# Edges of a GraphSAGE layer sorted into buckets in three parts of 32, 20 and 16 buckets a row instead of two of 41 and 27, with the sort in four portions and two parts merged under the sums

## The chip, the cores and the metric

The kernel runs on one core of a Trainium2 chip. The metric is the device time of one execution in microseconds (us); lower is better. The core's engines are called here as the profile calls them: PE (matmuls; PEld is its weight load), DVE (the vector engine), ACT (the scalar engine), POOL (GpSimd, which here issues the gathers) and SP (which issues most plain DMAs).

## The reference

```python
N, deg, D = 12500, 64, 64;  E = N * deg            # 800,000 edges
nsum = segment_sum(x[src], dst, N)                 # rows of x, added up by destination
return x @ w_self + (nsum * deg_inv[:, None]) @ w_neigh
```

`src` and `dst` are random and unordered, so the kernel has to bring the edges into an order in which TensorE can add them.

## The kernel before, in words

**Keys and sort.** Each edge becomes one 32-bit key (`make_keys`), made so that keys in order stand by bucket: a bucket is one block of 144 destinations (two halves of 72) and one of 98 blocks of 128 sources. There are 87 x 98 = 8526 buckets. The edges lie as 128 rows of 6250 keys, one row per lane. `sort_runs` sorts each row with a list of compare steps (`GAPS`): a minimum and a maximum on DVE per step (L223, L227; several instructions where the shape is ragged), and an ACT copy of the keys that have no partner (L229). The last 30 steps (`APART`) are cut into portions by position: keys below `SPLIT` first, then those below `CUT1`, then the rest.

**Rows and runs.** The buckets are cut into parts, each of 128 bucket rows: part 0 has 41 buckets a row, part 1 has 27 (`KPRS`). `find_rows` finds where each of a part's 128 bucket rows begins in each sorted row of edges, by one count over a window of keys for each (L454 on ACT with Sign and an accumulator, L456 on DVE, dealt out by `on_act`). The counts are made into offsets (L460, L461), transposed on PE (L463) and written as addresses `ix` (L465). With them `gather_runs` issues 128 indirect DMAs on POOL (L473), each followed by a short memset (`pause`), so that bucket row r lies in lane r as 128 sorted runs of `LENS[part][0]` keys. In part 0 the first `EARLY` = 76 counts stand between the second portion's steps.

**Merging.** `merge_runs` merges the 128 runs in seven rounds; `merge_round` issues its minima and maxima on DVE (L283, then L295 down the distances) with ACT copies of keys without a partner (L279). Part 0 is merged in groups of 32, 32 and 64 runs, the last round (`merge_last`, L312, L327, copies L316) in a lower and an upper piece, so that counting can begin below `LOWER`. Part 1's merge is a generator that the program advances by a number of ns, as an estimate, at a time.

**Buckets.** `find_buckets` and `count_below` find where each bucket begins in its row (part 0 on ACT, L610; part 1 on DVE, L612). `gather_buckets` brings each bucket of part 0 into 178 places `v` by indirect DMA (L633, addresses L644 on DVE); part 1 does the same under the sums (`find_and_gather`, addresses on ACT, L663). `decode_buckets` splits keys into source and destination (DVE, L680 to L685), narrows them to 16 bits (ACT, L690, L694), stores the sources to `sl` and turns the destinations into `dlT` (PE L700, ACT L701). Keys beyond a bucket's 128 places are collected by `leftovers`.

**The sums.** `nodes` runs over 1066 tiles of up to 8 buckets. For each 28 buckets `one_hots` broadcasts `sl` to all lanes (SP, L797, 896 KB) and DVE compares it: `ohs` (sources, L799) and `ohd` (destinations, L802). A tile has 8 matmuls `ct` = rows of x picked by `ohs` (L827), a copy `xg` of them to half precision (L837 on ACT, or L835 on DVE for some tiles from tile `SHARE` = 800), and 16 matmuls that add them by destination into PSUM `acc` (L883). Each 7 blocks of destinations the leftovers come in by one-hots `ohl` (L876) and the sum is copied out (L891, L893) and finished: `po` = sum @ w_neigh (L951), an ACT copy (L952), times the degree and plus the self terms on DVE (L957, L958), stored (L959). Between tiles the program issues the other streams: part 1's merge by 280 ns of estimate a tile, then one of its counts every second tile, then its decoding.

**Order.** `after_sort` and `sums_and_merge` write out this order by hand, and every engine takes its instructions in it. In the sums a DVE instruction thus stands behind all one-hots that the program wrote ahead of it; three `ohs`, five `ohd` and seven `xg` buffers say how far an engine may be ahead.

Of the kernel before, what the change touches and what calls it, by code (L numbers as in the profile page):

```python
# [23 lines left out]
H = 64  # L24
# [7 lines left out]
KPRS = (41, 27)  # L32
ROWS = (128, 128)
BASE = (0, 128 * KPRS[0])
NCOL = 128 * sum(KPRS)
NCNT = [(k + 3) // 4 for k in KPRS]
LENS = ((64, 108, 188, 336, 608, 1144, 2176, 4208),
        (48, 80, 132, 236, 420, 780, 1472, 2824))
# [12 lines left out]
SHARE = 800  # L51
EARLY = 76
SHARED = 0
SPLIT = 2560
# [3 lines left out]
LOWER = 2240  # L58
CLOSE = 32
BEHIND = 6  # L60
NEARLY = 36
LAG = 4
OCT = 7

# [17 lines left out]
class Windows:  # L82


    def __init__(self):
        cum = bid_cum()
        self.w1 = []
        for part in range(2):
# [8 lines left out]
        for part in range(2):  # L97
# [15 lines left out]
CUT1 = max(lo + 2 * n for lo, n in WIN.w1[:128]) + LENS[0][0] + 2  # L113
CUT1 += CUT1 % 2
FROM1 = min(lo for lo, _ in WIN.w1[128:]) - 2
assert max(lo + 2 * n for lo, n in WIN.w1[:EARLY]) <= SPLIT < CUT1 and FROM1 >= 0
# [4 lines left out]
def on_act(c):  # L121

    return c % 13 in (0, 2, 4, 7, 9, 11) or c < EARLY or c >= 128 + SHARED


def on_act2(part):

    return part == 0


def constants():
    thr = bid_base(np.concatenate([BASE[p] + np.arange(ROWS[p]) * KPRS[p] for p in range(2)]))
    act = np.array([on_act(c) for c in range(NC1)])
    t1 = np.where(act, -(thr - 1).view(np.float32), thr.view(np.float32))
    mul = np.where(act, -1.0, 2.0)
    add = np.array([(n if a else 0) + lo - 1 for (lo, n), a in zip(WIN.w1, act)])
    add[128:] -= FROM1
    c1 = np.zeros((128, 3, NC1), np.float32)
    c1[:, 0], c1[:, 1], c1[:, 2] = t1, mul, add
    out = {"c1": c1}  # L140
    for p in range(2):
# [3 lines left out]
        act = np.array([on_act2(p) for k in range(kpr)])  # L145
        first = np.array([lo + (n / 2 + 0.25 if a else 0) for (lo, n), a in zip(WIN.w2[p], act)])
        mid = v | np.uint32(1 << 14)
        c2 = out[f"c2_{p}"] = np.zeros((128, 5, kpr), np.float32)
# [3 lines left out]
        c2[:, 3] = np.where(act, -0.5, 1.0)  # L152
        c2[:, 4] = first + np.arange(128)[:, None] * PITCH2[p]
# [62 lines left out]
def sort_runs(nc, bufs, n):  # L216
# [19 lines left out]
    for last in (SPLIT, CUT1):  # L236
        edge = []
        for (gap, odd) in GAPS[:-APART - 1:-1]:
            last = -(-(last - odd * gap) // (2 * gap)) * 2 * gap + odd * gap
            edge.insert(0, last)  # L240
        edges.append(edge)
    edges = [[0] * APART] + edges + [[n] * APART]
    assert all(x < y for a, b in zip(edges, edges[1:]) for x, y in zip(a, b))
# [95 lines left out]
class Kernel:  # L339
    def __init__(self, tc, ctx, ins, outs):  # L340
# [4 lines left out]
        self.d1 = [self.dram.tile([128, n], F32, name=f"d1_{p}") for p, n in enumerate((CUT1, PITCH1 - FROM1))]  # L345
        self.sl = self.dram.tile([NCOL, 128], BF, name="sl")
        self.xt = self.dram.tile([NB * 128, 128], FH, name="xt")
        self.tops = [self.dram.tile([128, PCS * 9], F32, name=f"tops{p}") for p in range(2)]
        self.lt = [self.dram.tile([CHK, 128], F32, name=f"lt{p}") for p in range(2)]
        self.d2 = [self.dram.tile([128, PITCH2[p]], F32, name=f"d2_{p}") for p in range(2)]  # L350

    def setup(self):
        nc, keep = self.nc, self.keep
        self.c2 = [keep.tile([128, 5, KPRS[p]], F32, name=f"c2_{p}") for p in range(2)]
# [3 lines left out]
        self.cnt = keep.tile([128, sum(NCNT) + 3], F32, name="cnt")  # L358
        nc.gpsimd.memset(self.cnt, 0.0)
        self.deg = keep.tile([FB, 4 * NQ], F32, name="deg")  # L360
# [7 lines left out]
        for p in range(2):  # L368
# [7 lines left out]
        self.wide = keep.tile([128, OCT * HN], FH, name="wide")  # L376
        nc.gpsimd.iota(self.wide, pattern=[[1, OCT * HN]], base=0, channel_multiplier=0,
# [37 lines left out]
    def sort_edges(self, mps):  # L415
# [5 lines left out]
        self.c1 = l1.tile([128, 3, NC1], F32, name="c1")  # L421
        self.prow = [l1.tile([128, 128], F32, name=f"prow{p}") for p in range(2)]
        for p, n in enumerate((CUT1, PITCH1 - FROM1)):
# [6 lines left out]
        with tc.tile_pool(name="raw", bufs=1) as raw:  # L430
            with tc.manual_schedule():
                self.make_keys(raw, a)
                nc.sync.dma_start(self.c1, self.I["c1"])
                for p in range(2):
# [8 lines left out]
    def find_rows(self, part, mps):  # L443
# [3 lines left out]
        junks = [l1.tile([128, 512], BF, name=f"junk{e}") for e in "ad"]  # L447
        c0 = 128 * part
        for c in range(c0, c0 + 128):
# [3 lines left out]
            if on_act(c):  # L453
                nc.scalar.activation(junks[0][:, :n], w, AF.Sign, bias=self.c1[:, 0, c:c + 1], accum_out=a)  # L454
# [13 lines left out]
    def gather_runs(self, part, u):  # L468
# [3 lines left out]
        for p in range(128):  # L472
# [3 lines left out]
            self.pause(1 if part or p >= CLOSE else 2)  # L476

    def merge_runs(self, part, u, pong, sizes):
# [19 lines left out]
        first = 0  # L498
        for n in sizes:
# [5 lines left out]
            first += n  # L505
            while len(done) > 1 and done[-1][0] == done[-2][0]:
# [74 lines left out]
    def self_terms(self, pool, mps):  # L581
# [3 lines left out]
        for b0 in range(0, NB, 8):  # L585
# [8 lines left out]
            for j in range(nb // 2):  # L594
# [3 lines left out]
            nc.sync.dma_start(self.own[b0 * 128:(b0 + nb) * 128].rearrange("(b p) f -> p b f", p=128),  # L598
                              o[:, :nb // 2].rearrange("p a b f -> p (a b) f"))

    def count_below(self, part, k, acc):
# [5 lines left out]
        on = on_act2(part)  # L607
        junk = self.keep.tile([128, max(n for _, n in WIN.w2[0] + WIN.w2[1])], BF, name=f"junk2{part}")
        if on:
            nc.scalar.activation(junk[:, :n], w, AF.Sign, bias=c2[:, 2, k:k + 1], accum_out=acc[:, k:k + 1])  # L610
        else:
            nc.vector.tensor_scalar(junk[:, :n], w, c2[:, 1, k:k + 1], None, op0=OP.is_lt, op1=OP.add,  # L612
                                    accum_out=acc[:, k:k + 1])

    def find_buckets(self, part):
# [12 lines left out]
        nc.vector.tensor_tensor(acc, acc, self.c2[part][:, 3], op=OP.mult)  # L628
        nc.vector.tensor_tensor(acc, acc, self.c2[part][:, 4], op=OP.add)
# [18 lines left out]
    def find_and_gather(self, part, vp):  # L648
# [7 lines left out]
        for k in range(kpr + LAG):  # L656
# [4 lines left out]
            if k >= LAG:  # L661
                g = k - LAG
                nc.scalar.activation(ix[:, g:g + 1], acc[:, g:g + 1], AF.Relu, bias=self.c2[part][:, 4, g:g + 1])  # L663
# [3 lines left out]
    def decode_buckets(self, part, v, vp, mps):  # L667
# [5 lines left out]
        c0 = part * NCNT[0]  # L673
# [4 lines left out]
        def split(k, n, vk, _):  # L678
            vh = vk.rearrange("p k (h s) -> p k h s", h=2)
            nc.vector.tensor_tensor(vh, vh, bases(k, n, H), op=OP.bitwise_xor)  # L680
            w = vp.tile([128, 4, 128], I32, name="w", bufs=2 + 2 * part)[:, :n]
# [6 lines left out]
        def narrow(k, n, vk, w):  # L688
            l16 = vp.tile([128, 4, 128], BF, name="l16", bufs=4)
# [18 lines left out]
        per = 2 + 2 * part  # L708
# [329 lines left out]
    def after_sort(self, es, mps, aps):  # L1038
# [5 lines left out]
        with tc.manual_schedule():  # L1044
            low, mid, high = self.portions
            for step in low:
                step()
# [135 lines left out]
```

## Time and profile before

| what | value |
|---|---|
| runs without the profiler | 2067.23, 2072.83, 2077.07 us (median 2072.83) |
| profiled execution: time, span of its records | 2066.08 us, 2064.3 us |
| busy share of the span: DVE, ACT, PE, PEld, POOL | 90%, 64%, 50%, 43%, 29% |
| first one-hot of the sums on DVE | 994.44 us |
| DMA packets, bytes | 108362, 331.01 MB |
| PE's granted clock, mean | 0.993 |

A line of single instructions has the start, the duration in us, the engine, the line of the kernel, the operation, and output <- input with its shape; "x2" counts instructions of one kind in a row (the duration is then their sum), and what stands in brackets is the idle time ahead of it and what ended it. A line of a group has the number of instructions, their busy time in us, the mean ns of one, then the idle time of the engine just ahead of them by what ended it. PE's matmuls overlap, so its busy share isn't its peak.

### The profile page before, as it was taken

What the parts mean: (1) busy time and instruction counts of PE and PEld (TensorE: products, weight loads), DVE (VectorE), ACT (ScalarE), POOL (GpSimd) and SP (SyncE); (2) the same over time, 40 slices, a digit from 0 to 9 for tenths busy, and PEclk for the clock granted to TensorE, in tenths of its full rate; (3) what the DMA queues carried; (4) which work ended last, traced back from release to release, by engine and by line L of the source; (5) the groups of instructions that cost most, each with busy time, mean ns of one, the idle gap of its engine ahead of it and who ended that gap; (6) DMA issues with size and microseconds to landing.
All of it is one profiled execution on the core that took longest, in us unless ns stands there. A gap on an engine that the chain in (4) does not pass through costs nothing.

```text
span 2064.3 us, 59418 instructions
## 1 busy us (share of the span) xinstructions
PE 1026.0 (50%) x26057; PEld 885.5 (43%) x26057; DVE 1868.0 (90%) x1912; ACT 1318.7 (64%) x1920; POOL 593.4 (29%) x740
## 2 busy tenths in 40 slices
PE   0060000000000000000599999998879999999997
PEld 0050000000000000000588787887768888888886
DVE  8999999998999999899999998998987777798887
ACT  7470004603730000712699999998989999998896
POOL 1000000099899988478010010004400001000000
PEclk9999999999999999999999999999999999999999
DMA  4150000001000000112687887778767788777784
GB/s 149 54 113 11 0 0 26 16 14 44 21 20 17 15 18 16 49 37 59 233 278 267 283 281 260 281 287 279 280 234 287 275 293 298 280 294 295 277 305 170
DMA packets 108362, 331.01 MB, mean 160 GB/s; under 512 B 53696, under 2 KB 61840, under 8 KB 107584
## 3 DMA queue, kind: packets, MB, share of 16 engines
q1 hardware_dynamic: 90928, 306.89, 40.5%
q0 software_dynamic: 14352, 18.65, 4.2%
q8 instruction: 205, 3.36, 0.6%
q10 hardware_dynamic: 2816, 1.61, 0.3%
q14 instruction: 61, 0.50, 0.1%
HBM read 307.86 MB, written 19.23 MB: 158 GB/s over the span
## 4 chain that ended last, share of the span: by engine, by line
PE 37%; DVE 24%; POOL 21%; issue 10%; ACT 6%; DMA 1%; ACTq 0%; DVEq 0%; POOLq 0%; SPq 0%
PE ct L827 21%; POOL u L473 16%; PE acc L883 14%; DVE b L227 8%; DVE a L227 7%; ACT xg L837 4%; POOL pad L383 3%; DVE u L295 2%; POOL v L633 2%; DVE ohs L799 1%; DVE ohd L802 1%; PE po L951 1%; ACT junka L454 1%; PE pw L595 0%; ACT u L279 0%
## 5 line engine op out<-in xcount | busy, mean ns | idle before, releaser
L837 ACT ACTIVATE xg<-ct 128x1024 f16<-128x1024 f32 (+1 forms) x1028 | 966.9, 1130 | 73.7 <-PE ct L827 53.1
L827 PE MATMUL ct<-xh,ohs 128*128 128x128 f16 x8526 | 602.0, 221 | 41.8 <-ACT xg L837 17.4
L827 PEld LDWEIGHTS <-ohs 128*128 128x128 f16 x8526 | 497.7, 99 | 88.4 <-issue 36.9
L473 POOL DMA_INDIRECT u<-d,ix x256 | 340.8, 1331 | 404.2 <-DVE ix L465 363.8
L295 DVE TENSOR_TENSOR u<-u 128x512 f32<-128x512 f32 (+42 forms) x354 | 433.9, 1259 | 18.5 <-ACT u L279 11.4
L799 DVE TENSOR_SCALAR ohs<-slb,pidx 128x3584 f16<-128x3584 bf16 x305 | 350.9, 1151 | 96.4 <-PE ct L827 94.4
L883 PE MATMUL acc<-ohd,xg 64*128 64x72 f16 x17052 | 414.6, 194 | 39.8 <-issue 29.1
L883 PEld LDWEIGHTS <-xg 64*128 64x128 f16 x17052 | 325.5, 94 | 118.3 <-issue 38.6
L802 DVE TENSOR_TENSOR ohd<-iota,dlT 128x2016 f16<-128x2016 bf16 x305 | 366.3, 1201 | 0.0
L463 PE MATMUL stp<-idf,st 128*128 128x128 f32 x2 | 0.9, 447 | 440.7 <-DVE st L461 440.7
L227 DVE TENSOR_TENSOR b<-a 128x774 f32<-128x774 f32 (+45 forms) x154 | 211.3, 1420 | 4.2 <-ACT a L229 0.3
L700 PE MATMUL tr<-idb,l 128*128 128x128 bf16 x68 | 9.0, 271 | 385.3 <-ACT l L694 378.8
L227 DVE TENSOR_TENSOR a<-b 128x774 f32<-128x774 f32 (+41 forms) x140 | 194.8, 1436 | 4.0 <-ACT b L229 2.0
L279 ACT ACTIVATE u<-u 128x512 f32<-128x512 f32 (+15 forms) x67 | 42.7, 711 | 231.8 <-DVE u L283 210.5
L959 POOL DMA_DIRECT2D out<-o x24 | 26.2, 1092 | 571.7 <-DVE o L958 482.6
L463 PEld LDWEIGHTS stp<-idf,st 128*128 128x128 f32 x2 | 0.4, 182 | 441.2 <-issue 441.2
L700 PEld LDWEIGHTS <-l 128*128 128x128 bf16 x68 | 5.6, 116 | 388.8 <-ACT l L694 383.1
L229 ACT ACTIVATE a<-b 128x1 f32<-128x1 f32 (+44 forms) x57 | 23.4, 426 | 208.9 <-DVE b L227 208.9
L864 POOL DMA_INDIRECT lx<-xt,lxi x28 | 47.2, 1687 | 333.3 <-DVE lxi L862 156.1
L633 POOL DMA_INDIRECT v<-d,ix x68 | 104.3, 1534 | 80.6 <-DVE ix L644 40.0
L454 ACT ACTIVATE junka<-b,c 128x143 bf16<-128x143 f32 (+48 forms) x228 | 100.7, 442 | 25.5 <-DVE b L227 18.5
L283 DVE TENSOR_TENSOR u<-u 128x1024 f32<-128x1024 f32 (+17 forms) x48 | 73.0, 1556 | 11.6 <-DMA u<-d,ix 11.1
(135 smaller groups left out, 777.6 us busy)
## 6 DMA issues: line engine op xcount, KB each, us to landing
slb<-sl SPq DMA_DIRECT2D x305, 896.0 KB
u<-d,ix POOLq DMA_INDIRECT x256
xt<-xh SPq DMA_DIRECT2D x1, 3136.0 KB
own<-os SPq DMA_DIRECT2D x12, 256.0 KB
fo<-own SPq DMA_DIRECT2D x24, 126.0 KB
out<-o POOLq DMA_DIRECT2D x24, 126.0 KB
rd<-dst SPq DMA_DIRECT2D x4, 521.0 KB
rs<-src SPq DMA_DIRECT2D x4, 521.0 KB
```

The costliest lines, as they stand in the source:

```text
L227: nc.vector.tensor_tensor(view(dst, lo + sh, [[st, g], [1, l]]), x, y, op=op)
L283: nc.vector.tensor_tensor(at(oth, to, n), x, y, op=op)
L295: nc.vector.tensor_tensor(to, at(cur, ln + lo, n), at(cur, lo + k, n), op=op)
L383: self.nc.gpsimd.memset(self.pad, 0.0)
L454: nc.scalar.activation(junks[0][:, :n], w, AF.Sign, bias=self.c1[:, 0, c:c + 1], accum_out=a)
L473: nc.gpsimd.indirect_dma_start(out=u[:nr, p * w:(p + 1) * w], out_offset=None, in_=src, in_offset=bass.IndirectOffsetOnAxis(ap=self.start[ ...
L633: self.nc.gpsimd.indirect_dma_start(out=self.v[:, k].bitcast(F32), out_offset=None, in_=flat(self.d2[part], 128 * PITCH2[part]), in_offset ...
L799: nc.vector.tensor_scalar(s.rearrange("p c s -> p (c s)"), b, self.pidx[:, :1], None, op0=OP.is_equal)
L802: nc.vector.tensor_tensor(d, self.iota[:, None].to_broadcast([128, 14, HN, 2]), ix, op=OP.is_equal)
L827: nc.tensor.matmul(ct[:, i * 128:(i + 1) * 128], cols[i][0], self.xh[:, (b0 + i) % NB].rearrange("p a f -> p (a f)"), start=True, stop=True)
L837: nc.scalar.activation(xg[:, :cnt * 128], ct[:, :cnt * 128], AF.Copy)
L883: nc.tensor.matmul(acc[h][:, db % OCT * HN:(db % OCT + 1) * HN], xg[r, i * 128:(i + 1) * 128], d[r], start=db % OCT == 0 and sb == 0, stop ...
```

## The change

It touches most stages:

- Three parts: 32, 20 and 16 buckets a row, each of 128 rows (`KPRS`; `LENS` shorter to match). The sort is cut into four portions at `SPLIT` = 1672, 3266 and 5102 (before: 2560 and 4108).
- All counts of bucket rows and of buckets are ACT's (`on_act`, `on_act2` go). `EARLY` goes from 76 to 64. Part 1's row counts stand in the last portion and under part 0's merges, part 2's behind them.
- Part 0 is merged in groups of four times 32 runs. Part 1's first 96 run gathers come right behind part 0's run gathers, the other 32 behind part 0's bucket gathers; of its merge, up to 96 runs are grouped ahead of the sums, the rest under them. Part 2's 128 run gathers come one in every second tile of the sums, then its merge, counts and decoding.
- In the decoding, two fused instructions replace the xor, the count and the shift on DVE, and ACT does the count.
- The self terms are stored into `out` as well, early. The finish scales by the degree in four ACT copies instead of one, and adds to `out` with accumulating DMAs on POOL, without DVE.
- `ohl` is one instruction instead of two; `ohd` has four buffers and `xg` six. DVE takes `xg` copies once the last part is decoded, instead of from tile 800.

```diff
-KPRS = (41, 27)
+KPRS = (32, 20, 16)
+GROUPS = ((32, 32, 32, 32), (64, 32, 32), (128,))
+FIRST = 96
+FROM_TILE = (0, 60, 0)
+PACE = (0, 500, 420)
-SHARE = 800
-EARLY = 76
-SPLIT = 2560
+EARLY = 64
-LOWER = 2240
+LOWER = 1770
...
 # sort_runs
-    for last in (SPLIT, CUT1):
+    for last in [SPLIT] + CUT[:-1]:
...
 # find_rows
-            if on_act(c):
-                nc.scalar.activation(junks[0][:, :n], w, AF.Sign, bias=self.c1[:, 0, c:c + 1], accum_out=a)
-            else:
-                nc.vector.tensor_scalar(junks[1][:, :n], w, self.c1[:, 0, c:c + 1], None,
-                                        op0=OP.is_lt, op1=OP.add, accum_out=a)
+            nc.scalar.activation(junk[:, :n], w, AF.Sign, bias=self.c1[:, 0, c:c + 1], accum_out=a)
             yield c
-        nc.vector.tensor_tensor(st, acc, self.c1[:, 1, c0:c0 + 128], op=OP.mult)
-        nc.vector.tensor_tensor(st, st, self.c1[:, 2, c0:c0 + 128], op=OP.add)
+        nc.vector.tensor_tensor(st, self.c1[:, 1, c0:c0 + 128], acc, op=OP.subtract)
...
 # decode_buckets, split
-            nc.vector.tensor_tensor(vh, vh, bases(k, n, H), op=OP.bitwise_xor)
-            nc.vector.tensor_scalar(w.bitcast(F32), vk, 1 << 14, None, op0=OP.is_lt, op1=OP.add,
-                                    accum_out=self.cnt[:, c0 + k // 4:c0 + k // 4 + 1])
-            nc.vector.tensor_scalar(w, vk, 7, None, op0=OP.logical_shift_right)
+            for h in range(2):
+                nc.vector.scalar_tensor_tensor(w[:, :, at], vk[:, :, at], 7, base,
+                                               op0=OP.logical_shift_right, op1=OP.bitwise_xor)
...
 # narrow
+            nc.scalar.activation(self.junk()[:, :n * 128], w.rearrange("p k s -> p (k s)"), AF.Sign, bias=self.edge[:, :1], accum_out=self.cnt[:, c:c + 1])
...
 # finish
-            nc.scalar.activation(o[:n, at], po[:n, at], AF.Copy)
+                nc.scalar.activation(o[:n, b], po[:n, b], AF.Copy, scale=self.deg[:n, 4 * qq + b:4 * qq + b + 1])
-            nc.vector.tensor_tensor(o[:n, at], o[:n, at], dg, op=OP.mult)
-            nc.vector.tensor_tensor(o[:n, at], o[:n, at], own[:n, at], op=OP.add)
-            queue.dma_start(self.O["out"][r:r + nb * n].rearrange("(b p) f -> p b f", p=n), o[:n, b0:b0 + nb])
+                nc.gpsimd.dma_start(out, o[:n, at], accum_op=OP.add)
...
 # after_sort: part 0's rows and runs
-            for i, step in enumerate(mid):
+            for i, step in enumerate(portions[0]):
                 step()
-                while next(rows) + 1 < EARLY * (i + 1) // len(mid):
+                while next(rows) + 1 < EARLY * (i + 1) // APART:
                     pass
...
+            rows = self.find_rows(1, mps)
+            for step in last:
+                step()
+                for _ in range(2):
+                    next(rows)
...
 # sums_and_merge: the streams between tiles
+            if gathers and n % 2 and last != "gather" and self.picked < n - 1 and next(gathers, None) is None:
+                gathers = None
+            if change:
+                t += PACE[part]
+                while t > 0:
+                    if n < FROM_TILE[part] and self.grouped[part] >= FIRST:
+                        t = 0
+                        break
...
+                    last = next(change, None)
...
+                    t -= last
-            if merge:
-                t += 280
-                while merge and t > 0:
-                    dt = next(merge, None)
```

Where instructions stand now is shown for three places. The first is DVE where the second sorted portion ends. Before, these are the last of its row counts, the offsets of part 0 (`st`, `ix`) and the first steps of the third portion:

```order
L456 TENSOR_SCALAR junkd,acc_715<-b,c_107 128x218 x2
L456 TENSOR_SCALAR junkd,acc_715<-b,c_107 128x217 x2
L456 TENSOR_SCALAR junkd,acc_715<-b,c_107 128x216
L456 TENSOR_SCALAR junkd,acc_715<-b,c_107 128x215
L460 TENSOR_TENSOR st_905<-acc_715,c_107 128x128
L461 TENSOR_TENSOR st_905<-st_905,c_107 128x128
L465 SCALAR_TENSOR_TENSOR ix_910<-stp,prow_108 128x128
L227 TENSOR_TENSOR a<-b 128x16x53 x2
L227 TENSOR_TENSOR b<-a 128x22x41 x2
```

In the changed kernel (its own line numbers) DVE goes from the portion's last steps straight to the offsets, which need all 128 counts of ACT:

```order
L220 TENSOR_TENSOR a<-b 128x797 x2
L220 TENSOR_TENSOR b<-a 128x797 x2
L451 TENSOR_TENSOR st_930<-c_116,acc_741 128x128
L455 SCALAR_TENSOR_TENSOR ix_934<-stp,prow_117 128x128
L220 TENSOR_TENSOR a<-b 128x18x53 x2
L220 TENSOR_TENSOR b<-a 128x23x41 x2
L220 TENSOR_TENSOR a<-b 128x23x41 x2
L220 TENSOR_TENSOR b<-a 128x30x31 x2
```

So DVE's share of the row counts is gone from its row, and nothing has come in its place between the portion and the offsets.

The second place is DVE under the first sums. Before, one merge instruction (`u<-u`) of part 1 stands between two chunks of one-hots:

```order
L802 TENSOR_TENSOR ohd<-iota,dlT 128x2016
L295 TENSOR_TENSOR u<-u 128x2x689
L799 TENSOR_SCALAR ohs<-slb,pidx 128x3584
L802 TENSOR_TENSOR ohd<-iota,dlT 128x2016
L862 COPY lxi<-ls_3336 128x1
L295 TENSOR_TENSOR u<-u 128x2x748
L799 TENSOR_SCALAR ohs<-slb,pidx 128x3584
L802 TENSOR_TENSOR ohd<-iota,dlT 128x2016
```

In the changed kernel two or three of them stand there:

```order
L801 TENSOR_TENSOR ohd<-iota,dlT 128x2016
L288 TENSOR_TENSOR u<-u 128x16x32
L288 TENSOR_TENSOR u<-u 128x16x30
L288 TENSOR_TENSOR u<-u 128x16x34
L798 TENSOR_SCALAR ohs<-slb,pidx 128x3584
L801 TENSOR_TENSOR ohd<-iota,dlT 128x2016
L288 TENSOR_TENSOR u<-u 128x16x30
L288 TENSOR_TENSOR u<-u 128x16x32
```

They are smaller, each step (a minimum and a maximum) reads what the step ahead of it wrote, and the next chunk's one-hots wait behind them.

The third place is ACT while part 1's buckets are found under the sums. Before, only addresses (`ix`) and copies of finished sums (`o<-po`) stand between the copies `xg`, as DVE counts:

```order
L837 ACTIVATE xg<-ct 128x1024 x2
L663 ACTIVATE ix_1_14396<-acc_1_14395,c_1_71 128x1
L837 ACTIVATE xg<-ct 128x1024 x2
L952 ACTIVATE o<-po 126x256
L663 ACTIVATE ix_1_14396<-acc_1_14395,c_1_71 128x1
L837 ACTIVATE xg<-ct 128x1024 x2
```

In the changed kernel ACT also has the counts (`junk,acc`) and four smaller output copies:

```order
L836 ACTIVATE xg<-ct 128x1024
L608 ACTIVATE junk_10904,acc_1_10641<-u,c_1_75 128x288
L657 ACTIVATE ix_1_10642<-acc_1_10641,c_1_75 128x1
L836 ACTIVATE xg<-ct 128x1024 x2
L608 ACTIVATE junk_10970,acc_1_10641<-u,c_1_75 128x310
L657 ACTIVATE ix_1_10642<-acc_1_10641,c_1_75 128x1
L836 ACTIVATE xg<-ct 128x1024
L946 ACTIVATE o<-po,deg 126x64 x4
L836 ACTIVATE xg<-ct 128x1024
L608 ACTIVATE junk_11044,acc_1_10641<-u,c_1_75 128x329
```

The row of copies, which each tile needs, is now cut by two short instructions for every second tile.

More of the change, by code (lines that the diff above doesn't have):

```diff
@@ L497, in merge_runs @@
         done = []
-        first = 0
-        for n in sizes:
+        first = self.grouped[part] = 0
+        for n in GROUPS[part]:
             level, rs, nr = 0, lens[0], n
@@ L606, in count_below @@
         w = view(self.rows, lo, [[1, n]])
[L607 to L613, printed above, removed]
+        nc.scalar.activation(self.junk()[:, :n], w, AF.Sign, bias=c2[:, 2, k:k + 1], accum_out=acc[:, k:k + 1])
     def find_buckets(self, part):
@@ L1098, in sums_and_merge @@
                     counts = None
-        l2a.close()
+        other.close()
         vp = va.enter_context(tc.tile_pool(name="va", bufs=1))
         self.gather_buckets(0, vp)
+        for _ in gathers:
+            pass
+        ahead = self.ahead(merge)
         t = 0
-        while t < 8e3:
-            t += next(merge)
+        while t < 8e3 and next(ahead, None):
+            t += self.dt
         t = 0
@@ L1157, in run, with ahead @@
+        runs.close()
+    def ahead(self, merge):
+        size = sum(GROUPS[1][:-1])
+        while self.grouped[1] < size:
+            self.dt = next(merge)
+            yield True
     def run(self):
```

323 lines of the change are left out of this document (183 added, 140 removed).

## The prediction

> **What bounds the kernel now.** I read the page's busy line first, then a table of busy time cut at the program's stages, then single instructions.
>
> ```profile
> PE 1026.0 (50%) x26057; PEld 885.5 (43%) x26057; DVE 1868.0 (90%) x1912; ACT 1318.7 (64%) x1920; POOL 593.4 (29%) x740
> ...
> 412.00:889.00 477.00, 0.45 (x1) 0.18 (x1) 444.28 (x427) 137.53 (x415) 394.85 (x544) 1.00 0.09 23
> 889.00:994.40 105.40, 6.36 (x41) 3.54 (x41) 100.88 (x143) 25.51 (x38) 78.35 (x82) 1.00 0.21 60
> 994.40:1394.00 399.60, 368.05 (x9576) 318.18 (x9576) 379.10 (x371) 379.11 (x425) 29.96 (x16) 0.98 0.77 277
> 1394.00:1507.00 113.00, 93.52 (x2374) 79.65 (x2370) 101.52 (x159) 105.36 (x147) 47.72 (x39) 0.98 0.80 278
> 1507.00:1801.00 294.00, 279.21 (x7338) 240.43 (x7333) 219.90 (x260) 284.27 (x318) 17.23 (x15) 0.99 0.77 279
> 1801.00:2064.30 263.30, 240.52 (x6594) 211.62 (x6592) 227.51 (x241) 224.24 (x245) 18.60 (x16) 0.98 0.73 267
> ```
>
> After a stretch and its length stand PE, PEld, DVE, ACT and POOL, then PE's granted clock, the DMA share and GB/s. Up to 994.4 us the vector engine sorts and merges, 93 to 96% busy, and PE hardly works. Then come the sums: 1066 tiles of 24 matmuls each, so PE's count measures progress. 399 tiles take 399.6 us with DVE and ACT both 95% busy (one-hots and merges on the one, PSUM copies on the other); 99 tiles take 113.0 us while part 1 is found and decoded, ACT 93% busy; 306 take 294.0 us with ACT at 97%. Only in the last 263.3 us, where DVE takes some copies, do DVE and ACT drop to 86% and PE sets 0.92 us a tile. So DVE has no room before the sums and little in their first 400 us. The change takes merging out of the first half into the second, and moves counting from DVE to ACT.
>
> **Before the sums.**
>
> ```profile
> 392.35 1.84 DVE L227 TENSOR_TENSOR a<-b 128x774 f32<-128x774 f32 x2
> 394.23 1.84 DVE L227 TENSOR_TENSOR b<-a 128x774 f32<-128x774 f32 x2
> ...
> 396.17 0.48 ACT L454 ACTIVATE junka<-b,c 128x214 bf16<-128x214 f32 x1 [13.59 <-DVE b L227]
> 396.78 0.49 ACT L454 ACTIVATE junka<-b,c 128x215 bf16<-128x215 f32 x1
> ...
> 411.52 0.29 DVE L465 SCALAR_TENSOR_TENSOR ix<-stp,prow 128x128 uint32<-128x128 f32 x1 [0.63 <-PE stp L463]
> 491.07 2.37 DVE L283 TENSOR_TENSOR u<-u 128x1024 f32<-128x1024 f32 x2 [5.94 <-DMA u<-d,ix]
> 806.32 40.00 DVE L327 TENSOR_TENSOR u<-u 128x1203 f32<-128x1203 f32 x34 [0.38 <-ACT u L316]
> 851.50 6.63 DVE L283 TENSOR_TENSOR u<-u 128x3072 f32<-128x3072 f32 x2 [5.18 <-DMA u<-d,ix]
> 888.90 2.57 DVE L644 TENSOR_SCALAR ix<-acc 128x1 uint32<-128x1 f32 x41
> 994.44 1.15 DVE L799 TENSOR_SCALAR ohs<-slb,pidx 128x3584 f16<-128x3584 bf16 x1 [0.32 <-DMA slb<-sl]
> ...
> L633 POOL DMA_INDIRECT v<-d,ix x41: 949/1658/5363, 889.8 to 972.6; - x41
> L610 ACT ACTIVATE junk<-u,c 128x161 bf16<-128x161 f32 (+40 forms) x41 | 30.2, 735 | 26.1 <-DVE u L327 24.9
> L610 ACT ACTIVATION_READ_ACCUMULATOR junk<-u,c 128x1 f32 x41 | 7.6, 187 | 0.0
> ```
>
> *Sort.* It compares the same elements, in four portions with 60 more instructions. Two of 774 elements start every 1.88 us (392.35 to 394.23). Merges of few and of many elements differ by 0.96 elements a ns, which makes 1.61 us of it; the rest is 0.13 us an instruction. 60 x 0.13 = **+8**.
>
> *Row counts.* Now ACT stands idle for 13.59 us, then ACT and DVE share the last 52 counts: from the portion's end (396.1) to the offsets (411.5) pass 15.5 us. In the change all 128 are ACT's; 64 of them cannot start before the second portion is sorted, and DVE's next instruction needs the last one. At 0.61 us each (396.17 to 396.78) that is 39, and 2 to the offsets: 41 us with DVE idle, **+25.5**. Nothing stands ahead of that instruction on DVE that could hide it. The second portion ends some 26 us earlier, since its elements stand in later portions; so POOL's gathers still begin near 411, and DVE's merges come later. That removes the waits for gathered runs of 5.94 and 5.18 us: **-11**.
>
> *Merging part 0.* From 491.07 to 846.32 DVE needs 355.2 us for 324 instructions that the order counts, with 286,574 elements a lane (298.5 us): 0.175 us besides for each. The new order has 394 with 228,592 elements: 238 + 69 = 307, **-48**. ACT meanwhile has 196 row counts besides the short copies for which DVE waits; 0 to 15 us may be lost, I take **+2**, because ACT was 29% busy in this stretch.
>
> *Offsets of the buckets.* From 851.50 to 888.90 DVE has 37.4 us of work. Now the last 16 counts decide, at 0.92 us (735 + 187 ns): 15 to 16, and 2 to the offsets. **-19.5**.
>
> *To the first one-hot.* 105.5 us (888.90 to 994.44): 41 gathers start over 82.8 us, 2.07 each, and 21.8 us pass behind the last. With 32 gathers it is 31 x 2.07 + 22.7 = 87. **-18.5**.
>
> Together **-61.5** (the bounds of its parts -45 and -80): first one-hot near 933 us.
>
> **The sums.** A chunk is 28 buckets or 3.5 tiles.
>
> ```profile
> 1122.09 1.15 DVE L799 TENSOR_SCALAR ohs<-slb,pidx 128x3584 f16<-128x3584 bf16 x1
> 1123.15 1.20 DVE L802 TENSOR_TENSOR ohd<-iota,dlT 128x2016 f16<-128x2016 bf16 x1
> 1124.27 1.15 DVE L799 TENSOR_SCALAR ohs<-slb,pidx 128x3584 f16<-128x3584 bf16 x1
> ...
> 1126.45 1.76 DVE L295 TENSOR_TENSOR u<-u 128x1548 f32<-128x1548 f32 x1
> 1128.13 1.15 DVE L799 TENSOR_SCALAR ohs<-slb,pidx 128x3584 f16<-128x3584 bf16 x1
> ...
> 1421.69 0.30 ACT L663 ACTIVATE ix<-acc,c 128x1 uint32<-128x1 f32 x1
> 1421.87 1.94 ACT L837 ACTIVATE xg<-ct 128x1024 f16<-128x1024 f32 x2
> ...
> 1501.33 0.93 ACT L690 ACTIVATE l<-w 128x512 bf16<-128x512 int32 x1
> 1501.84 0.94 ACT L694 ACTIVATE l<-v 128x512 bf16<-128x512 int32 x1
> ...
> L837 ACT ACTIVATE xg<-ct 128x1024 f16<-128x1024 f32 (+1 forms) x1028 | 966.9, 1130 | 73.7 <-PE ct L827 53.1 <-DVE ohd L802 9.5 <-DVE ohs L799 4.6
> ```
>
> Start to start a chunk's one-hots cost DVE 1.06 + 1.12 = 2.18 us; a merge of 1548 elements costs 1.68, 0.07 more than its elements; a copy costs ACT 966.9/1028 = 0.94 us, an offset 0.18, a 512-element copy 0.51, and a count 0.43 and its elements at 1.2 a ns (0.61 at 214). The new order cuts the sums in five:
>
> *A, tiles 0 to 249.* DVE has 73 chunks (159) and 216 merges of part 1 with 94,936 elements (99). Beside them a merge costs 0.07 (between one-hots) to 0.175 (back to back, above); two or three stand in a row and each stage reads the one before, so I take 0.10: 22. With 7 us of short ones 287; ACT has 254. **DVE is the bound.**
>
> *B, to 322.5.* ACT has 73.5 copies (69), 20 counts with 7277 elements (14.7), 5 more of 512 in the decoding (4.3), 20 offsets (3.6), and 11 us of decoding and output copies: 103. DVE has 60.
>
> *C, to 655.* 95 chunks (207), 112 merges of part 2 with 120,716 elements (126 + 11) and 10 short: 354 on DVE; ACT 338.
>
> *D, to 721.5.* As B, with 66.5 copies, 16 counts with 6508 elements and 4 decoded groups: 90 on ACT.
>
> *E, the rest.* PE's pace: the last 263.3 us held 271 tiles, 73.5 more at 0.92 make 331.
>
> A bound engine isn't busy all the time; ACT reached 97% in the third stage. Dividing B and D by 0.965, A and C by 0.98 gives 293 + 106 + 361 + 93 + 331 = 1184 against 1069.9: **+114** (with 0.07 to 0.175 a merge 328 x -0.03 to +0.075, -10 to +25; with engines busy throughout -19).
>
> Edits at nothing: the second store of the self terms (DMA share 28% between 100 and 200 us); the accumulating output DMAs on POOL (under 11% busy in three of the four stages of the sums) in place of two DVE instructions; part 2's 128 run gathers, of which POOL can issue one every second tile. Uncovered, the last output DMA adds 2 us at the end.
>
> **Sum.** The profiled execution took 2066.08 us (span 2064.3), 6.75 under the median of the three runs. 2066.1 - 61.5 + 114 = **2118.6**; on the median's side a few us more, which I leave.
>
> **Rules of the Trainium skill.** "VectorE: DVE Perf Modes", section "The DRAIN you can't avoid", says that the next instruction doesn't start until the pipe is empty; the rows show 1.15 us one-hots followed after 1.06, so the measurement decides here; the rule's price is the second rival below. "DMA: Bandwidth & Descriptors", section "SWDGE vs HWDGE vs iDMA", says that DVE locks GpSimd out of descriptor writing while it uses both ports, which speaks against gathers under the one-hots; it is the fourth rival.
>
> ```profile
> L633 POOL DMA_INDIRECT v<-d,ix x27 | 35.1, 1299 | 34.4 <-ACT ix L663 18.0 <-DMA d<-u 14.2 <-issue 1.8
> L473 POOL DMA_INDIRECT u<-d,ix x256 | 340.8, 1331 | 404.2 <-DVE ix L465 363.8 <-issue 40.4
> ```
>
> **Rivals.** First, the other side: *the stages average out*. If an engine could work far ahead, the sums would take its whole load and not the sum of stage bounds. ACT's busy time is 993 us in the four rows; 36 counts (26), 9 in the decoding (8), copies for merges and outputs and the rest (33) and 10 fewer copies (-9) make 1051, at 0.965 1089: +19, total 2024. It decides from how far DVE may run ahead: three one-hot buffers are 10.5 tiles, the stages 66 to 333. For 2062 half of the 114 would have to go. Against it: 113.0 us for 99 tiles between two faster stages.
>
> Second, *a merge holds DVE for its whole duration* (1.76, not 1.68): 0.15 instead of 0.10 for 328, +16, total 2135. The one-hot rows speak against it; the back-to-back price of 0.175 speaks for it.
>
> Third, *counts overlap like copies* (0.94 against a duration of 1.13): only their elements cost. The wait of 39 becomes 11, B and D lose 45 x 0.43 = 19: total 2070. The start-to-start of 0.61 speaks against it.
>
> Fourth, *part 2's gathers come late*. They need 256 tiles at one per two; C starts at 322 near 1340 us. From 3 us apiece on C waits; at 4 us it would lose some 110, total 2230. Under the sums the 27 bucket gathers took 1.30 us against 1.33 for the run gathers ahead of them.
>
> **How the numbers follow.** Forecast 0.63 (2085 to 2150 with its bounds), averaging 0.11, whole durations 0.11, overlapping counts 0.12, late gathers 0.03. The range leaves out the late gathers, the averaging and the outer ends: 2065 to 2148. A measurement of this kernel tells about 0.5% from no change: faster by more 0.12, within 0.12, slower 0.76.
>
> **What would show it.** DVE idle for some 40 us, released by ACT, ahead of the first offsets; first one-hot near 933; tiles at 1.18 us in A and 1.09 in C with DVE at 97% or more; 1.4 us in B and D with ACT at 96%; 0.92 behind. I am wrong if A and C run at ACT's 1.0, or if the one-hots start before 910.

## The result, and the profile after

The changed kernel takes 2100.61 us (median of 4 runs, 2093.24 to 2103.31) against 2070.03 before: a ratio of 1.0144, 95% interval 1.0096 to 1.0191: slower by 1.4%. Measured again, with the kernel before on the same chip, it is 1.0158 (1.0132 to 1.0183). The forecast was 2118.6, in a range of 2065 to 2148. The profiled execution took 2093.24 us, 27.2 more than that of before; the forecast was 52.5 more.

The page's busy line, and the table of busy time, cut at the end of the row counts, at the end of part 0's merge, at the first one-hot and at the borders of the five stages A to E of the sums (columns as before):

```profile
PE 1060.4 (51%) x26074; PEld 913.7 (44%) x26074; DVE 1869.5 (89%) x2127; ACT 1440.1 (69%) x2455; POOL 822.5 (39%) x1003
```

```profile
0.00:409.00 409.00, 37.90 (x152) 31.85 (x152) 355.27 (x260) 178.56 (x397) 8.51 (x32) 1.00 0.22 54
409.00:818.70 409.70, 0.95 (x2) 0.36 (x2) 389.55 (x541) 172.90 (x629) 319.91 (x480) 1.00 0.09 21
818.70:909.40 90.70, 4.85 (x32) 2.74 (x32) 80.83 (x147) 40.41 (x85) 66.11 (x90) 1.00 0.26 70
909.40:1204.10 294.70, 247.53 (x6100) 214.63 (x6101) 288.95 (x399) 250.75 (x307) 270.02 (x284) 0.91 0.73 245
1204.10:1296.70 92.60, 72.53 (x1676) 60.31 (x1675) 56.98 (x66) 92.60 (x166) 54.47 (x51) 0.94 0.79 260
1296.70:1653.40 356.70, 319.90 (x8165) 276.46 (x8163) 354.21 (x352) 332.78 (x397) 40.90 (x19) 0.95 0.74 250
1653.40:1734.70 81.30, 62.36 (x1483) 51.78 (x1481) 52.30 (x65) 81.10 (x141) 25.90 (x24) 0.96 0.74 258
1734.70:2091.50 356.80, 314.38 (x8474) 275.60 (x8472) 291.45 (x304) 291.02 (x339) 36.62 (x25) 0.97 0.74 251
```

DVE's work is what it was: 1869.5 us busy against 1868.0. So 26 of the 27 us stand in DVE's idle time: 222 us (2091.5 - 1869.5) instead of 196. Divided at the first one-hot, this table and that of the prediction show where. Ahead of it DVE has 114 us less to do (825.7 busy instead of 939.9), but only 85 us are won (909.40 instead of 994.44), because it idles 84 us instead of 54: the first 409 us have 54 of the 84, where they had 17 before. In the sums DVE has 116 us more to do (1043.9 instead of 928.0), and they take 112 us more (1182.1 instead of 1069.9); its idle time there is 138 us, where it was 142. So in total what came under the sums was paid for in full.

Stage by stage, DVE is busy 98 and 99% of the time in A and C; in B and D it idles for 36 and 29 of 93 and 81 us, while ACT is busy without a break; in E it idles for 65.

The steps on DVE in front of the sums, as single instructions:

```profile
367.36 1.89 DVE L220 TENSOR_TENSOR b<-a 128x797 f32<-128x797 f32 x2
407.39 0.29 DVE L451 TENSOR_TENSOR st<-c,acc 128x128 f32<-128x128 f32 x1 [38.14 <-ACT junka L448]
408.31 0.29 DVE L455 SCALAR_TENSOR_TENSOR ix<-stp,prow 128x128 uint32<-128x128 f32 x1 [0.63 <-PE stp L453]
...
516.44 2.08 DVE L276 TENSOR_TENSOR u<-u 128x896 f32<-128x896 f32 x2
...
818.68 2.89 DVE L276 TENSOR_TENSOR u<-u 128x1280 f32<-128x1280 f32 x2
...
835.31 2.03 DVE L638 TENSOR_SCALAR ix<-acc 128x1 uint32<-128x1 f32 x32
...
909.40 1.19 DVE L798 TENSOR_SCALAR ohs<-slb,pidx 128x3584 f16<-128x3584 bf16 x1 [1.70 <-DMA slb<-sl]
```

The second portion ends at 369.3, and DVE stands still for 38.14 us until ACT has counted the rows. Nothing waits for gathered runs any more (5.94 and 5.18 us before).

### The profile page after: what moved, and what is told of

Same layout as the page of the kernel before. It is cut to its first block, busy times and chain, and to the rows that moved or that the text cites. A ratio compares the mean times of both kernels' runs of the same rounds, so it can differ in the third digit from the quotient of the medians.

```text
span 2091.5 us, 60398 instructions
## 1 busy us (share of the span) xinstructions
PE 1060.4 (51%) x26074; PEld 913.7 (44%) x26074; DVE 1869.5 (89%) x2127; ACT 1440.1 (69%) x2455; POOL 822.5 (39%) x1003
## 4 chain that ended last, share of the span: by engine, by line
DVE 47%; PE 22%; ACT 13%; issue 9%; POOL 6%; DMA 2%; ACTq 0%; DVEq 0%; SPq 0%; POOLq 0%
DVE u L288 15%; PE ct L826 13%; PE acc L880 8%; DVE b L220 7%; DVE ohd L801 6%; DVE a L220 6%; DVE ohs L798 5%; ACT xg L836 5%; POOL u L463 5%; DVE u L276 3%; ACT junka L448 2%; ACT junk L608 2%; DVE u L320 1%; ACT u L272 1%; DMA slb<-sl 1%
## 5 line engine op out<-in xcount | busy, mean ns | idle before, releaser
L836 ACT ACTIVATE xg<-ct 128x1024 f16<-128x1024 f32 x1017 | 968.5, 1101 | 90.1 <-PE ct L826 70.1
L463 POOL DMA_INDIRECT u<-d,ix x384 | 512.2, 1334 | 424.3 <-ACT junka L448 360.6
L826 PE MATMUL ct<-xh,ohs 128*128 128x128 f16 x8526 | 622.7, 226 | 73.9 <-ACT xg L836 37.9
L288 DVE TENSOR_TENSOR u<-u 128x496 f32<-128x496 f32 (+46 forms) x664 | 491.2, 772 | 24.3 <-ACT u L272 15.0
L952 POOL DMA_DIRECT2D out<-o x26 | 45.1, 1755 | 538.2 <-ACT o L946 521.1
L448 ACT ACTIVATE junka<-b,c 128x220 bf16<-128x220 f32 (+43 forms) x384 | 171.2, 446 | 100.4 <-DVE b L220 89.3
L220 DVE TENSOR_TENSOR b<-a 128x918 f32<-128x918 f32 (+50 forms) x184 | 214.7, 1214 | 4.8 <-ACT a L222 0.3
L220 DVE TENSOR_TENSOR a<-b 128x918 f32<-128x918 f32 (+47 forms) x170 | 198.3, 1210 | 4.5 <-ACT b L222 2.0
L378 POOL MEMSET pad<- 128x89 f32 x448 | 103.2, 230 | 2.0
L834 DVE CAST xg<-ct 128x1024 f16<-128x1024 f32 x52 | 63.5, 1223 | 43.8 <-PE ct L826 40.0
```

Source lines behind the costliest of these rows:

```text
L220: nc.vector.tensor_tensor(view(dst, lo + sh, [[st, g], [1, l]]), x, y, op=op)
L288: nc.vector.tensor_tensor(to, at(cur, ln + lo, n), at(cur, lo + k, n), op=op)
L378: self.nc.gpsimd.memset(self.pad, 0.0)
L448: nc.scalar.activation(junk[:, :n], w, AF.Sign, bias=self.c1[:, 0, c:c + 1], accum_out=a)
L463: nc.gpsimd.indirect_dma_start(out=u[:nr, p * w:(p + 1) * w], out_offset=None, in_=src, in_offset=bass.IndirectOffsetOnAxis(ap=self.start[ ...
L826: nc.tensor.matmul(ct[:, i * 128:(i + 1) * 128], cols[i][0], self.xh[:, (b0 + i) % NB].rearrange("p a f -> p (a f)"), start=True, stop=True)
```

## The experiments

The theory after the result: the change costs what DVE, and behind it ACT, stand idle for in single places, namely the row counts and the short stages B and D; and a merge under the sums is paid in full as long as DVE bounds the stage. Ratios are to the kernel before, run beside each kernel on the same chip, with their intervals; the changed kernel's own is 1.0158. Times "less than the changed kernel" are differences of these ratios, 0.01 being 20.7 us.

**The wait for the row counts.**

```diff
-            for _ in rows:
-                pass
+            for _ in range(128 - EARLY):
+                next(rows)
+            for step in portions[1][:17]:
+                step()
+            assert next(rows, None) is None
...
-            for step in portions[1]:
+            for step in portions[1][17:]:
```

> Edit: seventeen steps of the third sorted portion stand between the second portion and part 0's offsets. Theory (DVE's idle time is the loss): the 38.1 us that DVE waits for the row counts go, POOL's gathers still begin near 409, merging starts near 479 instead of 516.4, the first one-hot comes near 873 instead of 909.4, and the time falls by 36 us (profiled execution 2093.2 to about 2057). Rival (POOL's pace): the runs that the merges need come no earlier, the wait only moves to the gathered runs (waits of over 20 us by DVE for them), and the time falls by less than 15.

Ratio 0.9980 (0.9956 to 1.0005), 37 us less than the changed kernel. On DVE:

```profile
404.26 2.14 DVE L220 TENSOR_TENSOR a<-b 128x917 f32<-128x917 f32 x2
407.95 0.29 DVE L451 TENSOR_TENSOR st<-c,acc 128x128 f32<-128x128 f32 x1 [1.55 <-ACT junka L448]
...
478.47 1.43 DVE L220 TENSOR_TENSOR b<-a 128x574 f32<-128x574 f32 x2
479.81 2.08 DVE L276 TENSOR_TENSOR u<-u 128x896 f32<-128x896 f32 x2
```

The wait is 1.55 us, the merge begins at 479.81 with no wait for runs, and the first one-hot at 872.1, 37.3 earlier. The rival (POOL's pace) falls.

**The merges under the sums.**

```diff
-PACE = (0, 500, 420)
+PACE = (0, 378, 420)
```

> Edit: part 1's merge is spread over the first 332 tiles of the sums instead of 250. Theory (DVE is the bound of that stage, ACT close behind): the stage takes about 342 us for 332 tiles (1.03 a tile instead of 1.18), the tiles saved at the end would have cost 0.97 to 1.0 each, and the time falls by 30 us. Rival (buffers, PE or DMA set the pace there, not the merges): the tiles stay near 1.18 us as long as merges last, and the time rises by 15 us or stays.

Ratio 1.0034 (1.0009 to 1.0058), 26 us less. Stage A of this kernel, with 335 tiles by the count of PE's matmuls instead of 254:

```profile
908.80:1259.10 350.30, 316.85 (x8046) 271.95 (x8046) 343.33 (x450) 326.39 (x400) 290.91 (x309) 0.97 0.80 270
```

It takes 1.045 us a tile instead of 1.158, with DVE still 98% busy and ACT now 93%. So the merges set the pace. Spread thinner, they cost less in all: the 81 tiles more make the stage 55.6 us longer, 0.69 each, since the merges stay the same and DVE, its bound, has only those tiles' one-hots to add. The last stage, with 84 tiles fewer, is 75.0 us shorter, 0.89 each.

**The short stages.** First, DVE copies while a part is found and decoded:

```diff
-            if vector and turn % 2:
+            if vector and (turn % 2 or self.finding):
...
-            pend.append(gather(b0, cnt, self.changed))
+            pend.append(gather(b0, cnt, self.changed or self.finding))
...
+                    self.finding = last in ("gather", "tile")
```

> Edit: while a part's buckets are found and decoded under the sums, DVE takes one copy of a tile's rows for each chunk of one-hots (some 40 copies in all), as it does in the last stage. Theory (ACT is the bound of these two stages, DVE has room): they take 78 and 70 us instead of 96 and 86 for the same tiles, and the time falls by 30 us. Rival (the stages go by a gather or a decoding step for every second tile, or by PE, whose clock was 0.95 there): the tiles stay at 1.3 us and the time doesn't change by more than 8 us.

Ratio 1.0122 (1.0078 to 1.0166): 7 us less, which the intervals don't tell from nothing. The profile shows the stages themselves as the theory had them:

```profile
1203.70:1283.40 79.70, 65.02 (x1677) 55.45 (x1675) 76.17 (x82) 75.81 (x146) 54.63 (x50) 1.00 0.89 292
1283.40:1645.20 361.80, 319.33 (x8168) 274.79 (x8166) 357.60 (x357) 332.28 (x395) 47.40 (x21) 0.96 0.74 249
1645.20:1715.70 70.50, 59.45 (x1480) 50.59 (x1479) 65.18 (x70) 66.48 (x123) 29.37 (x24) 0.98 0.81 282
1715.70:2080.40 364.70, 316.10 (x8472) 276.75 (x8469) 297.48 (x317) 290.38 (x338) 39.37 (x25) 0.96 0.73 249
```

B falls by 12.9 and D by 10.8, but C and E take 5 and 8 us more than in the profile above. DVE has 3.4 and 6.0 us more to do in them (357.60 and 297.48 us busy): with copies to make in B and D, it leaves some of its other work there for later (E has one chunk of one-hots more, D one less). Of 24 us won, 11 are left in the profiled execution (2080.4 to 2091.5) and fewer in the medians. Second, this part of the change undone: the bucket counts of parts 1 and 2 are DVE's again.

```diff
-        nc.scalar.activation(self.junk()[:, :n], w, AF.Sign, bias=c2[:, 2, k:k + 1], accum_out=acc[:, k:k + 1])
+        if part:
+            nc.vector.tensor_scalar(self.junk()[:, :n], w, c2[:, 1, k:k + 1], None, op0=OP.is_lt, op1=OP.add,
+                                    accum_out=acc[:, k:k + 1])
+        else:
+            nc.scalar.activation(self.junk()[:, :n], w, AF.Sign, bias=c2[:, 2, k:k + 1], accum_out=acc[:, k:k + 1])
...
```

> Edit: one part of the change undone, the bucket counts of parts 1 and 2 are DVE's again (36 counts under the sums); nothing else. Theory (these counts on ACT, the bound engine of the two short stages, are a cost of the change): the stages take 79 and 70 us instead of 92.6 and 81.8, and after what the other stages give back the time falls by 8 to 20 us. Rival (PE or the steps of the program set the pace there): both stages and the time stay within 5 us.

Ratio 1.0082 (1.0056 to 1.0107), 16 us less (10 in the profiled execution, where A, C and E are 6.5, 1.5 and 4.1 us longer): B 82.2 us, D 69.4. So counting on ACT was the wrong side in these two stages.

**Together.** All three edits:

> Edit: the three of before together (steps of the third portion under the row counts, part 1's merge over 332 tiles, DVE copies while buckets are found and decoded). Theory (the three take away DVE's and ACT's waits at different places, so they add up): 37 + 23 + 12 to 24 us less than the changed kernel on this chip, a ratio of 0.975 to 0.985 to the kernel before. Rival (they share one gain, since the tiles that become faster are the same): not under 0.99.

Ratio 0.9774 (0.9747 to 0.9802): 2020.61 us, 79 less than the changed kernel and 2.3% under the kernel before. They add up (37 + 26 + 7 to 24). Its busy line:

```profile
PE 1040.8 (52%) x26074; PEld 896.5 (44%) x26074; DVE 1896.6 (94%) x2153; ACT 1416.4 (70%) x2429; POOL 829.8 (41%) x1003
```

DVE is idle for 123 us of 2019.9 instead of 222 of 2091.5. And with the counts on DVE as a fourth edit:

> Edit: the three edits of the combined kernel and the counts on DVE as well. Theory (ACT still bounds the two short stages of the combined kernel at 1.13 us a tile, PE would allow 1.0): they come to 1.0 to 1.05 a tile, and the time falls by 6 to 14 us against the combined kernel, a ratio near 0.972 to the kernel before. Rival (PE, with its own stalls, is the bound there by now): no change, 0.977.

Ratio 0.9882 (0.9832 to 0.9932): 22 us worse than the three. Both ways of relieving ACT at once overshoot. Stage B:

```profile
1234.10:1319.70 85.60, 68.05 (x1714) 57.66 (x1706) 82.87 (x119) 66.82 (x107) 33.67 (x29) 0.98 0.80 266
```

DVE is now busy 97% of the time and ACT 78%: the bound has changed sides. Stages B and D make up 12 of the 25 us that the profiled execution lost; A and C are 7 and 3 us longer too, and why was not tried.

**What a gather costs on POOL.** The change's 32 bucket gathers started 1.73 us apart, not 2.07 as the 41 before.

```diff
-GROUPS = ((32, 32, 32, 32), (64, 32, 32), (128,))
+GROUPS = ((32, 32, 32, 32), (32, 32, 32, 32), (128,))
-PACE = (0, 500, 420)
+PACE = (0, 575, 420)
```

> Edit: part 1 is merged in four groups of 32 runs instead of 64, 32 and 32, so that the merges beside part 0's bucket gathers have 640 elements and fewer instead of up to 1280; as many tiles as before carry the rest. Theory (an indirect DMA's issue on POOL lasts until the DVE instruction beside it ends): a bucket gather ahead of the sums starts every 1.5 us instead of 1.73, and the 32 take 47 us instead of 54. Rival (a gather's cost is its own, DVE has no part in it): 1.7 us each as before. The time moves by less than 10 us either way, since there are more merge instructions.

The groups of these gathers on POOL, of the kernel before, the changed one and this one:

```profile
L633 POOL DMA_INDIRECT v<-d,ix x41 | 69.3, 1689 | 46.2 <-DVE ix L644 40.0 <-issue 5.8 <-DVE v L680 0.3
```

```profile
L627 POOL DMA_INDIRECT v<-d,ix x32 | 43.3, 1352 | 73.9 <-DVE ix L638 69.1 <-issue 4.6 <-DVE u L276 0.2
```

```profile
L627 POOL DMA_INDIRECT v<-d,ix x32 | 35.0, 1093 | 68.8 <-DVE ix L638 64.1 <-issue 3.2 <-DVE u L288 1.1
```

With the start to start (2.07, 1.73, 1.46 us) goes the mean length of the DVE merges beside them: 2.12, 0.90 and 0.51 us. The shortest gather takes 0.95 us in all three. Single instructions show why, a merge and a gather of the changed kernel, then a count on DVE and a gather of the one before:

```profile
854.76 1.03 DVE L288 TENSOR_TENSOR u<-u 128x848 f32<-128x848 f32 x1
855.31 1.30 POOL L627 DMA_INDIRECT v<-d,ix  x1 [0.16 <-issue]
```

```profile
928.46 0.69 DVE L682 TENSOR_SCALAR_CACHE_REDUCE w<-v 128x512 f32<-128x512 int32 x1
928.47 0.95 POOL L633 DMA_INDIRECT v<-d,ix  x1 [0.16 <-DVE v L680]
```

The merge ends at 855.79 and the gather 0.82 us later, at 856.61. Beside the count, which has one input, the gather takes its 0.95. Of the 105 gathers in these three groups, 69 start while a merge runs that has more than 0.13 us to go. Of these, 65 end 0.81 to 0.84 us behind the end of that merge, three end later still, and one isn't held. So the rival falls, and the theory holds but for these 0.82 us: a gather that starts beside a merge is held until the merge has ended.

The 32 gathers take 45 us, yet the first one-hot comes only 2.0 us earlier (907.37): behind the start of the last gather pass 27.3 us instead of 19.5. From the offsets to the first one-hot DVE is busy for 92, 96 and 90% of the time (changed kernel, the one before, this one):

```profile
835.30:909.40 74.10, 4.85 (x32) 2.74 (x32) 68.19 (x134) 24.56 (x51) 66.11 (x90) 1.00 0.29 75
```

```profile
888.90:994.40 105.50, 6.36 (x41) 3.54 (x41) 100.98 (x143) 25.51 (x38) 78.35 (x82) 1.00 0.21 60
```

```profile
834.00:907.30 73.30, 4.86 (x32) 2.75 (x32) 66.12 (x171) 25.58 (x58) 64.61 (x99) 0.50 0.29 79
```

So faster gathers alone win little there, as long as DVE has the same merges and decoding to do. The time rose, to 1.0275 (1.0217 to 1.0332), 24 us more, where I expected under 10. Stage A has 13 of them (308 us instead of 295): DVE bounds it, and the smaller groups need 254 merge instructions there instead of 216. The rest lies in the later stages, and why was not tried.

**The last stage.** E took 356.8 us for 346 tiles (by its `ct` matmuls), the forecast was 331 for 344.5. Five runs ask why: both kernels again on one chip, the output stored without accumulation, fewer matmuls of leftovers, and the kernel before with the change's buffers.

> No edit: the changed kernel again, beside the kernel before on one chip, to measure the ratio more closely and to have a trace of it from the chip of the next runs. Expected: a ratio of 1.010 to 1.019. If the longer last stage (1.03 us a tile against 0.975 before) belongs to the change, it is as long here in this trace and not in that of the kernel before; if it belongs to the chip or to chance, both move together.

> No edit: one look at the kernel before, on the same chip, for the pace of its last 270 tiles. If the change makes the last stage slower: 0.975 us a tile again. If chip or chance does: 1.01 or more.

```profile
1737.00:2097.50 360.50, 316.94 (x8472) 277.89 (x8469) 292.13 (x309) 290.80 (x339) 39.10 (x26) 0.96 0.74 249
```

```profile
1801.00:2069.20 268.20, 239.17 (x6554) 210.27 (x6546) 226.56 (x240) 222.95 (x243) 17.41 (x16) 0.99 0.72 261
```

By matmuls (24 a tile) that is 1.02 us a tile here for the changed kernel and 0.98 for the one before: the change's last stage is slower on one chip too. Over the same tiles, from the 797th on by the starts of their `ct` matmuls, it is 0.984 against 0.960 here, and 0.978 against 0.938 in the first two profiles.

```diff
-                nc.gpsimd.dma_start(out, o[:n, at], accum_op=OP.add)
+                nc.gpsimd.dma_start(out, o[:n, at])
```

> Edit: the finished sums are stored by plain DMAs from POOL, not accumulating ones (the self terms are left out of the output). Theory (the accumulating stores cost nothing but at the end): the time falls by 0 to 5 us, all of it behind the last tile. Rival (they hold up the sums through the DMA engines, which were 84% busy where they fell): the tiles of the last stage take 0.975 us instead of 1.03, 15 to 20 us less.

The last stage takes 360.4 us, ratio 1.0153 (1.0119 to 1.0187): no difference that counts. Behind the last output copy pass 9.7 us (2094.1 - 2084.4) instead of 10.3 on the same chip.

```diff
-                for i, (m, x) in enumerate(ohl):
+                for i, (m, x) in list(enumerate(ohl))[-1:]:
```

> Edit: of the pieces of leftover edges that each 7 blocks of destinations add, only the last is added on PE (the others are left out of the output; their one-hots are still made). Theory (three parts have more such pieces, and their matmuls on PE are part of what makes the last stage longer): the last stage takes 9 us less than 360. Rival (PE's stalls have other causes): it stays within 4 us.

The last stage takes 368.2 us, ratio 1.0157 (1.011 to 1.0205): not shorter. But it is a small test: the edit takes away 22 of this stage's 32 matmuls of leftovers, and all 32 are 7.2 us of PE's time in the changed kernel.

```diff
-            d = pool.tile([128, 14, HN, 2], FH, name="ohd", bufs=5)
+            d = pool.tile([128, 14, HN, 2], FH, name="ohd", bufs=4)
-            xg = pool.tile([128, 1024], FH, name="xg", bufs=7)
+            xg = pool.tile([128, 1024], FH, name="xg", bufs=6)
```

> Edit: the kernel before with the change's buffers alone, four for the destinations' one-hots instead of five and six for the copied rows instead of seven. Theory (fewer buffers are why the last stage is slower in the change): its tiles from 1806 us on take 0.985 us instead of 0.95, the last stage is about 10 us longer, and the other stages of the sums, ACT-bound, stay. Rival (the buffers decide nothing, the last stage's extra time is from elsewhere): the time stays within 5 us of the kernel before.

Ratio 0.9990 (0.9965 to 1.0015), last stage 267.7 us: the buffers are not it, in the kernel before. Of the 26 us over the forecast, 5 are the end: behind ACT's last output copy pass 10.8 us instead of 5.9, where the last store is POOL's and was SP's (that queue wasn't tried alone).

```profile
2079.82 0.89 ACT L946 ACTIVATE o<-po,deg 126x64 f32<-126x64 f32 x4 [1.38 <-PE po L943]
```

```profile
2058.23 0.21 ACT L952 ACTIVATE o<-po 26x64 f32<-26x64 f32 x1 [0.38 <-PE po L951]
```

Some 6 come from my rate: I took 0.92 us for the added tiles, where the stage's own average was 0.96 to 0.98, and the first 76 tiles of E took 1.00 (1.05 in the second profile). Another 10 or so are the last 270 tiles, at 0.978 instead of 0.938. Why both are slower stays open.

## Why the prediction was right, point by point

The sign and the mechanism held: DVE bounds A and C, ACT bounds B and D, and the gain before the sums is smaller than what the sums lose. The size did not: +27 us came of a forecast +52.5. Against the profiled execution (2093.24) the forecast is 25 us too high, almost all of it before the sums: -85.0 instead of -61.5.

| term | forecast, us | measured, us | from |
|---|---|---|---|
| sort | +8 | +7.7 | DVE up to 516.44 less the gap for the row counts, against 485.1 less its own |
| row counts | +25.5 | +23.6 | 39.3 from the portion's end to the next step, 15.7 before |
| waits for gathered runs | -11 | -11.1 | none left |
| merging part 0 | -46 | -53.0 | 818.68 - 516.44 = 302.2, 355.2 before |
| offsets of the buckets | -19.5 | -20.8 | 835.31 - 818.68 = 16.6, 37.4 before |
| gathers to the first one-hot | -18.5 | -31.4 | 909.40 - 835.31 = 74.1, 105.5 before |
| A, B, C, D, E | 293, 106, 361, 93, 331 | 294.7, 92.6, 356.7, 81.3, 356.8 | the table of stages |

**The step that was mis-sized most** is the last one ahead of the sums: "31 x 2.07 + 22.7 = 87", where 74.1 were measured. I took a gather's 2.07 us as its own price. It measured 1.73, because the merges beside it had become shorter, and by my sum that is 10.5 of the 12.9 us. But the sum itself is in doubt: the run with still shorter merges shows 1.46, which by the sum is 8.4 us, and the first one-hot came 2.0 us earlier. What I left out is DVE's own work in this stretch. It fell by 32.8 us (100.98 to 68.19), and the stretch by 31.4. That DVE's work decides it is argued from these shares, not shown. The second is merging, 7 us better. By my own mark, one-hots before 910, this part was wrong: they start at 909.40.

In the Trainium skill, "SBUF — State Buffer", section "Who interferes with whom", says that a DVE instruction with two inputs in SBUF contends with a GpSimd instruction that reads SBUF, not with one that only writes it; my prediction cited another page for DVE's two-port modes alone. The same section infers why a `tensor_tensor` did not stall a DMA in a probe. Here merges of that kind, with two inputs, did hold the gathers (65 of 69, above), so for these indirect DMAs the measurement decides. Whether it is the reading of their addresses `ix` that waits, and which port is taken, no run here shows.

In the sums +112.2 stand against +114, but that is luck: errors cancel. A and C came within 2% of the one-hot and merge prices; DVE was 98 and 99% busy, as said. B and D were 25 us shorter together: ACT was busy without a break there and I had allowed it 96.5%, and PE saw only 69 and 61 tiles in them, not 72.5 and 66.5. E was 26 us longer: its first 76 tiles took 1.00 us instead of my 0.92, the others 0.978 instead of 0.938, and the end 5 us more (I had said 2, and the sum for E leaves them out).

The rivals: averaging over the stages would have given +19 for the sums, they show +112. Counts that overlap like copies would have made DVE's wait 11 us, it was 38.14. Whole durations for the merges would have made A and C together 16 us longer than the forecast 654; they took 651. Part 2's gathers were nearly late: the last starts at 1294.2, part 2's first merge at 1300.67, without a wait.

## What to carry to other kernels

When work moves from one stage to another, add up the busy and the idle time of the bounding engine by stage: here its work was the same to 2 us, the sums grew by what it got to do in them, and ahead of them a new wait took back a good part of what was saved. The places had cheap covers: independent steps of the sort put ahead of the waiting instruction, a lower rate of merges, a few copies or the counts on the other engine. An engine that is relieved hands its bound to its neighbour: two reliefs of ACT that each shortened B and D left the combined kernel 22 us slower together than one of them alone. Moving work under a stage is free only as far as that stage's engine has room, so spread it as thinly as the deadline allows.

## What the runs showed of the hardware

An indirect DMA's issue on POOL took 0.95 us at the least and on the average 1.09, 1.35 and 1.69 us beside DVE merges of 0.51, 0.90 and 2.12 us. One that started while a merge ran ended 0.81 to 0.84 us behind the merge (65 of 69); beside a count with one input it took its 0.95.

PE's granted clock in stretches without matmuls differed from run to run and decided nothing: the changed kernel's four runs, of 2093.24, 2103.31, 2101.27 and 2099.96 us, had mean clocks of 0.971, 0.972, 0.787 and 0.973. In the combined kernel it was 0.50 from 409 to 782 us, with 0.95 to 1.00 in the sums; in the changed kernel 1.00 in the same stretch. So the mean clock of a run (0.798 and 0.971 here) says little where PE idles long.

```profile
409.00:782.00 373.00, 0.95 (x2) 0.36 (x2) 353.43 (x508) 173.70 (x633) 325.76 (x480) 0.50 0.10 23
```
